# Block 1's stores of split weights: every other one issued by ScalarE instead of SyncE

## The chip, the cores and the metric

The kernel runs on one core of one Trainium2 chip. The metric is the device time of one execution in microseconds (us). Five engines work side by side, each through its own instruction stream in order: PE (TensorE, matmuls), DVE (VectorE), ACT (ScalarE), POOL (GpSimd) and SP (SyncE, which here does nothing but issue DMAs). DMAs can be issued from SP, ACT and POOL; they run on 16 DMA engines.

## The reference

```python
q_s = softmax of q over its 64 channels;  k_s = softmax of k over the 576 positions
kv  = einsum('bhsd,bhse->bhde', k_s, v)          # 8 batches x 8 heads, 64x64 each
x   = einsum('bhsd,bhde->bhse', q_s, kv)         # then laid out as (4608, 512)
xn  = x / sqrt(mean(x*x) + 1e-6) * rms_g
g   = xn @ w_gate;  val = xn @ w_val             # 512 -> 1536
out = (silu(g) * val) @ w_out                    # 1536 -> 512, float32
```

Inputs and output are float32: q, k and v of shape (8, 8, 576, 64), two weights of 512x1536 and one of 1536x512.

## The kernel before

The 4608 tokens are worked in nine blocks of 512. Blocks 0, 1 and 2 run one after the other with plain matrix products; the other six run as three pairs with Strassen products. In a plain block the hidden width of 1536 is cut into 12 chunks of 128. A chunk has a number s = 12 x block + i, so block 1 is s = 12 to 23. Steps of a chunk are `f1.s` (gate and value products, PE, line 973), `g_mul`, `silu`, `h_mul` (DVE, ACT, DVE), `h_hi` and `h_lo` (the split of the hidden values in two, ACT and POOL or DVE) and `f2.s` (the output product, PE, line 1010). Between them stand the steps of the attention of a later batch: `q_load`, `k_load`, `v_load` fetch a group of q, k or v (8, 3 and 5 DMAs), `q_max` to `q_x` are the softmax of q and its product with kv, `k_max` to `kv_lo` the softmax of k and kv.

Every float32 factor is split into a high and a low part, and a product is three products of parts. For the weights this is `w_hi`, `w_lo`, `o_hi`, `o_lo` (high parts are ACT casts, line 408; low parts are subtractions on POOL or DVE, lines 897 and 905). The split halves of a chunk lie in a ring of two tiles `w` (gate and value halves, 1 MB) and two tiles `o` (output halves, 512 KB). For the Strassen products sums of weight quarters S1 to S4 are made in block 1 also (`s_add.i.n`) and split (`s_hi`, `s_lo`, line 955) into a ring of three tiles `parts`.

In block 1 all these halves are written to DRAM, to be loaded back from block 2 on by POOL (`w_back`, `o_back`, `w_in`, `o_in`) in place of being split again: `w_keep.s` stores 1 MB (12 times), `o_keep.s` 512 KB (12 times) and `s_keep.i.n` 512 KB (24 times). They are the stores of the change. `r_keep` stores raw weights likewise and stays on SP.

What sets the order: a list of steps written out as text, `ORDER` (lines 22 to 341), worked through once by a loop at the end of the kernel. A step "name.arguments:engine" calls the function of that name; `unit[0]` is the engine that stands behind the colon, and `on(default)` gives it or the function's default. Each engine's stream is the list's order, cut to that engine's instructions. Nothing is reordered later; waits are put in from the tiles that an instruction reads and writes.

The DMAs of SP and of ACT count on eight semaphores, DMAHW0 to DMAHW7, handed out nearly in turn in the order of the list. An issuing instruction first waits until the DMA that used its semaphore last has landed. So no more than eight of these DMAs are under way, and a DMA on one engine can wait for one that the other engine has to issue. POOL's DMAs have semaphores of their own.

Of the kernel before, what the change touches and what calls it, by code (L numbers as in the profile page):

```python
# [90 lines left out]
kv_lo.2.0 w_lo.14.1:P f1.14.0 o_lo.15:D q_rec.2.1 s_lo.1.2:D k_tr.2.2 q_x.2.0 q_mul.2.1:P q_sum.2.3 k_top.2.2 o_keep.15
v_ones.2.3 s_add.0.1:D k_rows.2.2 f1.14.1 w_keep.14 q_t.2.1 q_mul.2.2:P v_load.2.3 q_hi.2.1:A s_add.2.1:D o_hi.13:A
k_sub.2.2 q_lo.2.1:P h_hi.13:A q_half2.2.3 s_hi.0.1:A q_x.2.1 o_lo.13:P w_hi.15.0.2:A q_sum2.2.3 q_rec.2.3 x_hi.2.1:A
s_add.2.2:D x_sq.2.0 x_lo.2.1 h_lo.13:P f2.13 x_hi.2.0:A g_mul.14 k_exp.2.2 o_keep.13 w_lo.15.0:P x_lo.2.0 s_hi.2.1:A
q_load.3.0 q_t.2.2 k_mm.2.2 q_mul.2.3:P k_max.2.3 q_hi.2.2:A x_sq.2.1 w_lo.15.1:P f1.15.0 q_t.2.3 silu.14 v_ones.3.0
s_lo.2.1:D s_lo.0.1:P h_mul.14 k_tr.2.3 s_keep.1.2 k_load.3.0 k_top.2.3 f1.15.1 h_hi.14:A s_add.0.3:D o_hi.14:A
q_lo.2.2:D w_hi.16.0.2:A w_keep.15 o_lo.14:P g_mul.15 s_keep.0.1 k_eps.2.2 r_keep.0 k_rec.2.2 kv_hi.2.2:A x_acc.2.1:D
o_keep.14 k_rows.2.3 h_lo.14:P f2.14 s_hi.2.2:A kv_lo.2.2 q_load.3.2 q_hi.2.3:A q_max.3.0 silu.15 w_lo.16.1:P k_sub.2.3
q_half.3.0 k_exp.2.3 w_lo.16.0:P f1.16.0 k_max.3.0 s_lo.2.2:P h_mul.15 q_max2.3.0 h_hi.15:A q_lo.2.3:P k_tr.3.0
w_hi.17.0.2:A q_x.2.2 k_top.3.0 g_mul.16 k_rows.3.0 s_hi.0.3:A w_lo.17.0:P f1.16.1 w_keep.16 s_keep.2.1 v_load.3.0  # L100
q_sub.3.0:D k_sub.3.0 q_exp.3.0 w_lo.17.1:D k_exp.3.0 k_mm.2.3 s_add.2.4:D x_sq.2.2 s_lo.0.3:D silu.16 h_lo.15:D f2.15
s_add.0.2:D q_max.3.2 x_hi.2.2:A s_add.0.4:P s_keep.2.2 q_sum.3.0 f1.17.0 o_hi.16:A s_keep.0.3 h_mul.16 o_hi.17:A
o_lo.16:P k_load.3.1 s_hi.0.4:A k_eps.2.3 q_half.3.2 w_hi.18.0.2:A o_lo.17:P k_rec.2.3 q_half2.3.0 kv_hi.2.3:A f1.17.1
q_sum2.3.0 x_lo.2.2 h_hi.16:A s_add.3.1:P o_keep.16 w_keep.17 q_rec.3.0 kv_lo.2.3 q_load.3.1 q_mul.3.0:P s_hi.3.1:A
g_mul.17 silu.17 k_mm.3.0 s_lo.0.4:P q_t.3.0 s_hi.0.2:A q_x.2.3 k_eps.3.0 v_ones.3.2 h_lo.16:D f2.16 k_max.3.1
w_lo.18.0:P x_hi.2.3:A x_lo.2.3 w_lo.18.1:P v_ones.3.1 s_lo.0.2:D f1.18.0 o_keep.17 k_rec.3.0 s_lo.3.1:P h_mul.17
s_keep.0.4 kv_hi.3.0:A k_load.3.2 h_hi.17:A x_acc.2.2:D h_lo.17:P x_sq.2.3 f1.18.1 g_mul.18 w_hi.19.0.2:A w_keep.18
s_keep.3.1 x_acc.2.3:D v_load.3.1 q_max.3.1 w_lo.19.0:P n_hi.2:A o_hi.18:A q_half.3.1 k_tr.3.1 silu.18 f2.17 o_lo.18:P
q_max2.3.1 s_hi.2.4:A k_top.3.1 h_mul.18 n_lo.2:P h_hi.18:A w_hi.20.0.2:A w_lo.19.1:D f1.19.0 kv_lo.3.0 s_add.2.3:P
w_keep.19 k_max.3.2 s_keep.0.2 h_lo.18:P s_hi.2.3:A o_keep.18 v_load.3.2 o_hi.20:A k_rows.3.1 w_lo.20.0:D k_tr.3.2  # L110
f1.19.1 k_sub.3.1 s_add.3.2:P g_mul.19 s_lo.2.4:P k_top.3.2 silu.19 n_sum.2 q_sub.3.1:P h_mul.19 k_rows.3.2 f2.18
h_hi.19:A w_lo.20.1:D k_exp.3.1 q_max2.3.2 n_t.2 s_keep.2.4 q_sub.3.2:P q_load.3.3 n_y0.2 o_lo.20:P n_y1.2 q_exp.3.1
f1.20.0 s_hi.3.2:A w_hi.21.0.2:A k_sub.3.2 o_hi.19:A w_lo.21.0:P q_sum.3.1 q_exp.3.2 k_mm.3.1 k_exp.3.2 q_half2.3.1
s_add.1.3:P w_keep.20 f1.20.1 q_hi.3.0:A o_keep.20 q_sum2.3.1 v_ones.4.0 s_add.4.3:D v_load.4.0 k_eps.3.1 o_lo.19:P
k_rec.3.1 g_mul.20 kv_hi.3.1:A k_mm.3.2 q_sum.3.2 h_lo.19:P silu.20 n_cols.1 f2.19 k_eps.3.2 q_half2.3.2 q_lo.3.0:P
k_rec.3.2 h_mul.20 w_lo.21.1:P q_sum2.3.2 kv_lo.3.1 h_hi.20:A o_keep.19 f1.21.0 kv_hi.3.2:A k_load.4.0 v_ones.3.3
s_lo.3.2:D w_hi.22.0.2:A n_rows.2 s_lo.2.3:P s_hi.1.3:A w_keep.21 q_max.3.3 o_hi.21:A q_rec.3.1 s_keep.2.3 h_lo.20:D
f1.21.1 s_keep.3.2 q_mul.3.1:P n_cols.2 k_load.3.3 q_half.3.3 w_lo.22.1:P q_max2.3.3 g_mul.21 q_t.3.1 w_lo.22.0:P f2.20
kv_lo.3.2 q_hi.3.1:A s_lo.1.3:D silu.21 w_keep.22 q_load.4.0 q_lo.3.1:D o_lo.21:D q_x.3.0 h_mul.21 f1.22.0 s_add.4.1:D
h_hi.21:A s_add.3.3:D w_hi.23.0.2:A h_lo.21:P s_hi.4.1:A o_hi.22:A q_sub.3.3:P q_x.3.1 g_mul.22 f1.22.1 k_max.3.3  # L120
o_lo.22:P silu.22 s_keep.1.3 x_sq.3.1 o_keep.21 k_max.4.0 x_sq.3.0 s_hi.3.3:A q_exp.3.3 q_rec.3.2 w_lo.23.0:D f2.21
s_lo.4.1:D x_acc.3.1:D s_keep.4.1 w_hi.24.0.2:A s_add.3.4:D v_load.3.3 w_lo.23.1:D s_hi.3.4:A f1.23.0 q_sum.3.3
s_add.5.3:P o_hi.23:A h_mul.22 q_half2.3.3 q_mul.3.2:P h_hi.22:A q_max.4.0 s_lo.3.4:P w_keep.23 f1.23.1 q_sum2.3.3
q_t.3.2 o_keep.22 q_half.4.0 q_hi.3.2:A q_load.4.1 s_add.5.1:P g_mul.23 q_lo.3.2:D h_lo.22:D f2.22 x_cp.3.0:A
w_lo.24.0:D x_cp.3.1:A o_lo.23:D silu.23 s_lo.3.3:D q_rec.3.3 k_tr.3.3 w_lo.24.1:D q_x.3.2 o_keep.23 s_hi.5.1:A
# [13 lines left out]
g_mul.27 f1.27.1 k_max.4.2 silu.27 k_load.4.3 v_ones.4.3 s_lo.4.4:P q_half2.4.2 v_load.4.3 n_lo.3:P k_eps.4.1 k_rec.4.1
q_t.4.1 kv_hi.4.1:A f2.26 w_lo.28.0:P h_mul.27 x_sq.4.0 kv_lo.4.1 q_hi.4.1:A s_lo.5.4:D o_hi.27:A h_hi.27:A q_sum2.4.2  # L140
w_lo.28.1:D s_keep.5.4 w_hi.29.0.2:A n_sum.3 q_max2.4.3 q_rec.4.2 q_load.5.1 q_sub.4.3:P k_tr.4.2 f1.28.0 k_top.4.2
n_t.3 q_mul.4.2:P q_exp.4.3 h_lo.27:D q_lo.4.1:P n_y0.3 s_hi.5.3:A k_rows.4.2 f1.28.1 k_sub.4.2 s_keep.4.4 o_lo.27:P
q_t.4.2 r_keep.3 k_exp.4.2 q_sum.4.3 q_load.5.0 w_lo.29.0:P q_half2.4.3 q_x.4.1 g_mul.28 w_back.30 f2.27 x_sq.4.1
k_max.4.3 s_lo.5.3:P x_cp.4.1:A silu.28 n_y1.3 w_lo.29.1:P s_keep.5.3 k_tr.4.3 f1.29.0 q_sum2.4.3 q_rec.4.3 h_mul.28
q_mul.4.3:P k_top.4.3 h_hi.28:A n_rows.3 o_hi.28:A h_lo.28:P q_t.4.3 o_hi.29:A k_mm.4.2 q_hi.4.2:A o_lo.28:P k_rows.4.3
k_eps.4.2 k_load.5.0 f1.29.1 g_mul.29 k_rec.4.2 k_sub.4.3 silu.29 x_nm.3.0:P kv_hi.4.2:A q_load.5.2 k_exp.4.3 kv_lo.4.2
v_ones.5.1 f2.28 q_max.5.0 w_back.31 q_lo.4.2:P q_half.5.0 q_hi.4.3:A q_max2.5.0 q_max.5.1 x_acc.4.1:P q_half.5.1
# [197 lines left out]
def linear_attention_then_gated_ffn(ctx: ExitStack, tc, q, k, v, w_gate, w_val, w_out, rms_g, out):  # L345
    nc = tc.nc
# [568 lines left out]
    def w_keep(s):  # L915
        i, odd = divmod(s % NF, 2)
        nc.sync.dma_start(parts_of(i, A21 if odd else A11, 2),
                          wh_[s].rearrange("p m a b f -> p m a (b f)").bitcast(F32))
# [508 lines left out]
```

## Time and profile before

| | us |
|---|---|
| median of three runs | 946.04 (943.25 to 947.05) |
| the profiled execution | 943.55 |
| its span, first to last instruction | 941.8 |
| busy: PE / DVE / ACT / POOL | 921.6 / 726.2 / 470.3 / 539.3 |
| block 1's stores lie between | 144 and 316 |

The profile is of one execution. Its span lacks 1.75 us of that execution's time, and that execution is 2.5 us below the median. The granted TensorE clock was 0.997 over the span. All numbers below are in us from the span's start unless said otherwise. "SPq" and "ACTq" are the issuing of DMAs on SP and ACT, which counts as no busy time.

### The profile page before, as it was taken

How to read it: one execution, taken by the hardware profiler on the slowest of the kernel's cores; microseconds unless marked ns; L12 is line 12 of the kernel's file. 1: busy time of each engine (PE TensorE's matmuls, PEld its weight loads, DVE VectorE, ACT ScalarE, POOL GpSimd, SP SyncE). 2: the span in 40 equal slices, each digit the busy share in tenths (PEclk: the TensorE clock that was granted, in tenths of full speed). 3: DMA queues.
4: the chain of work that ended last, by engine and by line, in shares of the span. 5: the costliest groups of instructions: out<-in, count | busy, mean ns of one | idle time of the engine just before them, and what ended most of it. 6: DMA issues, size and time to landing. Idle time of an engine off the chain costs nothing.

```text
span 941.8 us, 14388 instructions
## 1 busy us (share of the span) xinstructions
PE 921.6 (98%) x4625; PEld 748.3 (79%) x4625; DVE 726.2 (77%) x1525; ACT 470.3 (50%) x745; POOL 539.3 (57%) x531
## 2 busy tenths in 40 slices
...
GB/s 248 293 241 214 155 42 281 299 251 270 316 260 166 243 239 297 201 226 244 256 188 266 254 280 201 294 317 252 173 185 220 195 209 269 269 206 205 49 134 90
DMA packets 215463, 211.79 MB, mean 225 GB/s; under 512 B 139828, under 2 KB 176732, under 8 KB 210780
## 3 DMA queue, kind: packets, MB, share of 16 engines
...
q14 instruction: 38, 0.31, 0.1%
...
## 4 chain that ended last, share of the span: by engine, by line
PE 82%; DVE 5%; DMA 5%; SPq 4%; POOL 1%; issue 1%; ACT 1%; DVEq 0%; ACTq 0%; POOLq 0%
PE ps_gv L1122 18%; PE ps_gv L973 13%; PE ps_o L1122 12%; PE ps_o L1010 7%; PE ps_a L1122 7%; PE ps_o L1331 6%; PE ps_o L1215 4%; PE ps_a L1331 3%; PE ps_gv L1331 3%; DMA qt<-in_q_dram 2%; PE ps_a L1215 2%; PE ps_gv L1215 2%; PE ps_a L577 2%; PE ps_a L785 1%; DMA od<-o 1%
## 5 line engine op out<-in xcount | busy, mean ns | idle before, releaser
L973 PE MATMUL ps_gv<-xh,w 128*128 128x512 f32 x576 | 190.2, 397 | 3.6 <-DVE gs L985 2.9
L1122 PE MATMUL ps_gv<-x,ring 128*128 128x512 f32 x576 | 143.0, 393 | 0.0
L973 PEld LDWEIGHTS ps_gv<-xh,w 128*128 128x128 f32 x576 | 108.3, 188 | 28.8 <-DVE gs L985 4.1
L1122 PEld LDWEIGHTS ps_gv<-x,ring 128*128 128x128 f32 x576 | 107.0, 188 | 22.3
L973 PE MATMUL ps_gv<-xl,w 128*128 128x512 f32 x288 | 111.7, 391 | 0.0
L1143 DVE TENSOR_TENSOR tmp<-tmp,ps_gv 128x512 f32<-128x512 f32 x84 | 57.2, 683 | 47.8 <-PE ps_gv L1122 43.9
L1122 PE MATMUL ps_o<-x,ring 128*128 128x512 f32 x360 | 85.0, 390 | 0.0
L1095 POOL DMA_DIRECT2D ring<-wd x54 | 30.8, 570 | 88.9 <-PE ps_gv L1122 39.6
L1122 PEld LDWEIGHTS ps_o<-x,ring 128*128 128x128 f32 x360 | 67.6, 188 | 14.2
L1010 PE MATMUL ps_o<-o,hh 128*128 128x512 f32 x288 | 73.9, 398 | 0.1
L973 PEld LDWEIGHTS ps_gv<-xl,w 128*128 128x128 f32 x288 | 54.2, 188 | 10.6 <-issue 0.4
L1010 PEld LDWEIGHTS ps_o<-o,hh 128*128 128x128 f32 x288 | 52.7, 188 | 11.4 <-POOL o L905 0.4
L408 ACT CAST hh<-gs 128x512 fp32r<-128x512 f32 x50 | 30.8, 617 | 49.8 <-POOL gs L1287 19.7
L1143 DVE TENSOR_TENSOR tmp<-tmp,ps_o 128x512 f32<-128x512 f32 x42 | 28.7, 685 | 25.5 <-PE ps_o L1122 25.1
L897 POOL TENSOR_TENSOR w<-w,w 128x512 fp32r<-128x512 f32 x34 | 44.7, 1325 | 4.3 <-ACT w L408 2.4
L994 POOL TENSOR_TENSOR hl<-gs,hh 128x512 fp32r<-128x512 f32 x23 | 32.0, 1391 | 21.5 <-ACT hh L408 15.3
L534 DVE TENSOR_REDUCE cm<-kt 116x128 f32<-116x640 f32 x28 | 36.6, 1311 | 5.1 <-DMA kt<-in_k_dram 4.9
L1010 PE MATMUL ps_o<-o,hl 128*128 128x512 f32 x144 | 39.0, 393 | 0.0
L1122 PE MATMUL ps_a<-x,ring 128*128 128x512 f32 x144 | 37.0, 392 | 0.0
L1122 PE MATMUL ps_a<-x,w 128*128 128x512 f32 x144 | 36.7, 390 | 0.0
L1095 POOL DMA_DIRECT2D w<-wd x18 | 10.1, 562 | 45.5 <-PE ps_a L1122 35.7
L1122 PE MATMUL ps_gv<-x,w 128*128 128x512 f32 x144 | 35.1, 392 | 0.0
...
## 6 DMA issues: line engine op xcount, KB each, us to landing
...
```

The source lines that it names most:

```text
L408: (e.copy if e is nc.scalar else e.tensor_copy)(dst, src)
L534: nc.vector.tensor_reduce(out=cm, in_=kt_[b, g].rearrange("p h j d -> p h d j"), axis=AX.X, op=ALU.max)
L577: nc.tensor.matmul(pk[h * D:(h + 1) * D, :D + 1], lhsT=ke[:n, h, j], rhs=vt[:n, j, h], start=(j == 0), stop=(j == len(rows) - 1))
L897: on(nc.gpsimd).tensor_tensor(out=w[:, :, 1], in0=halves(s % NF, a, 1)[:, 0], in1=w[:, :, 0].bitcast(F32), op=ALU.subtract)
L973: nc.tensor.matmul(pd[s], lhsT=w[:, a, c // 2, m, c % 2 * P:c % 2 * P + P], rhs=X[j, c][x], start=(n == 1), stop=(n == 3 * NKT))
L994: on(nc.gpsimd).tensor_tensor(out=hl, in0=g_[s], in1=h_[s][0].bitcast(F32), op=ALU.subtract)
L1010: nc.tensor.matmul(po[t], lhsT=a[:, t * P:(t + 1) * P], rhs=w, start=(i == 0 and n == 0), stop=(i == NF - 1 and n == len(terms) - 1))
L1095: nc.gpsimd.dma_start(t, src.rearrange("p a b f -> p (a b f)"))
L1122: nc.tensor.matmul(abc[p, i, m, b], lhsT=src[:, h, c * P:(c + 1) * P], rhs=operand(o, c, x), start=first and n == 0, stop=n == 5, skip_gro ...
L1143: nc.vector.tensor_tensor(out=dst, in0=ux[u + (src,)], in1=abc[u + (b,)], op=ALU.add)
L1215: nc.tensor.matmul(pa[p, t, k], lhsT=a[:, k * P:(k + 1) * P], rhs=w, start=(c == 0 and n == 0), stop=(c == NF - 1 and n == 2))
L1331: nc.tensor.matmul(qacc[p, b, x], lhsT=ws[l][x], rhs=h[m], start=first and i == 0 and n == 0, stop=i == NH - 1 and n == 2, skip_group_chec ...
```

## The change

The engine table gets an entry for SP, the three store functions take the engine that their step names, and the 48 store steps of block 1 are tagged `:A` (ACT) and `:S` (SP) in turn. A tag moves the instruction into ACT's stream at the place of the step. 24 stores are ACT's now: 8 of `w_keep` (12, 14, 16, 18, 19, 20, 22, 23), 7 of `o_keep` (12, 16, 17, 18, 19, 21, 23) and 9 of `s_keep` (1.4, 1.2, 0.1, 2.2, 2.3, 3.4, 5.1, 4.2, 4.4), 16 MB of 30 MB together.

```diff
-    where = {"A": nc.scalar, "D": nc.vector, "P": nc.gpsimd, "": None}
+    where = {"S": nc.sync, "A": nc.scalar, "D": nc.vector, "P": nc.gpsimd, "": None}
...
     def w_keep(s):
         i, odd = divmod(s % NF, 2)
-        nc.sync.dma_start(parts_of(i, A21 if odd else A11, 2),
+        on(nc.sync).dma_start(parts_of(i, A21 if odd else A11, 2),
...
     def o_keep(s):
-        nc.sync.dma_start(od[s % NF], ot_[s].bitcast(F32))
+        on(nc.sync).dma_start(od[s % NF], ot_[s].bitcast(F32))
...
     def s_keep(i, n):
-        nc.sync.dma_start(parts_of(i, {1: S1, 2: S2, 3: S3, 4: S4}[n], 1)[:, :, 0],
+        on(nc.sync).dma_start(parts_of(i, {1: S1, 2: S2, 3: S3, 4: S4}[n], 1)[:, :, 0],
```

In `ORDER` the store steps and some loads stand at other places of the text, but the instructions of PE, DVE and POOL keep their order, and so do those of ACT apart from the stores that it gains. SP keeps the order of its loads; a few of the stores that it keeps stand one or two loads earlier or later. Line numbers of the changed kernel are one higher.

First place, SP before, from the store of chunk 14's output halves (od_113) over the eight DMAs of `q_load.3.2` to the stores of `w_keep.16` and `s_keep.2.1` (both wd_107):

```order
L1231 DMA rd_123<-w_92 256x1x512 [waits DMAHW7_49]
L921 DMA od_113<-o 128x1024 [waits DMAHW0_49,Pool_49]
L647 DMA qt<-in_q_dram 32x6x32 [waits DMAHW1_49,DVE_49]
...
L647 DMA qt<-in_q_dram 32x10x32 [waits DMAHW6_49]
L647 DMA qt<-in_q_dram 32x10x32 [waits DMAHW7_49]
L647 DMA qt<-in_q_dram 32x10x32 [waits DMAHW0_49]
L917 DMA wd_107<-w 128x2x1024 [waits DMAHW1_49,Activation_49,Pool_49]
L958 DMA wd_107<-parts 128x2x512 [waits DMAHW2_49,DVE_49]
L523 DMA vt<-in_v_dram 112x5x64 [waits DMAHW3_49]
```

The same place of SP in the change:

```order
L1232 DMA rd_123<-w_92 256x1x512 [waits DMAHW0_49]
L922 DMA od_113<-o 128x1024 [waits DMAHW1_49,Pool_49]
L648 DMA qt<-in_q_dram 32x6x32 [waits DMAHW3_49,DVE_49]
...
L648 DMA qt<-in_q_dram 32x10x32 [waits DMAHW7_49]
L648 DMA qt<-in_q_dram 32x10x32 [waits DMAHW0_49]
L648 DMA qt<-in_q_dram 32x10x32 [waits DMAHW1_49]
L648 DMA qt<-in_q_dram 32x10x32 [waits DMAHW2_49]
```

And ACT there in the change, where `w_keep.16` and `s_keep.2.2` (wd_107) now stand:

```order
L983 ACTIVATE gs<-gs 128x512
L570 ACT_TABLE_LOAD [waits DMAHW7_49,DMAHW6_49]
L570 ACTIVATE kt<-kt 116x640 [waits DVE_49]
L918 DMA wd_107<-w 128x2x1024 [waits DMAHW7_49,Activation_49,Pool_49]
L409 CAST hh<-gs 128x512 [waits DVE_49]
L959 DMA wd_107<-parts 128x2x512 [waits DMAHW2_49,Pool_49]
L409 CAST w<-w_94 128x4x256 [waits DMAHW6_49,PE_49]
```

Before, the 1 MB store stood on SP behind the q load, and `s_keep.2.2` further back behind a v load. Now both are ACT's, ahead of its cast `hh`. They use DMAHW7 and DMAHW2, and the q load's fifth and eighth DMA wait on these two semaphores; before, the eighth waited for the store od_113.

Second place, ACT in the change around `s_keep.4.4` (wd_109), behind the silu of chunk 27:

```order
L983 ACT_TABLE_LOAD
L983 ACTIVATE gs<-gs 128x512 [waits DVE_49]
L959 DMA wd_109<-parts 128x2x512 [waits DMAHW5_49,Activation_49,Pool_49]
L414 ACTIVATE kv<-ps_a,rs 64x64 [waits DVE_49,PE_49]
L414 ACTIVATE kv<-ps_a,rs 64x64
```

And SP in the change at the three DMAs of `k_load.4.3`, the v load behind them, a store and the first of `q_load.5.1`:

```order
L526 DMA vt<-in_v_dram 1x2x64 [waits DMAHW3_49]
L499 DMA kt<-in_k_dram 112x2x320 [waits DMAHW4_49,PE_49,Activation_49]
L499 DMA kt<-in_k_dram 3x2x320 [waits DMAHW5_49]
L500 DMA kt<-in_k_dram 1x10x64 [waits DMAHW6_49]
L524 DMA vt<-in_v_dram 112x5x64 [waits DMAHW7_49]
...
L959 DMA wd_110<-parts 128x2x512 [waits DMAHW4_49,DVE_49,Activation_49]
L648 DMA qt<-in_q_dram 32x10x32 [waits DMAHW5_49,Pool_49]
```

The store takes DMAHW5 on ACT, and the second DMA of the k load, SP's, is the next to use it. Before, `s_keep.4.4` stood on SP, behind `q_load.5.1` and ahead of `q_load.5.0`.

More of the change, by code (lines that the diff above doesn't have):

```diff
@@ L91 @@
[L91 to L125, printed above, removed]
@@ L126 @@
-q_mul.3.3:P q_max2.4.0 k_top.3.3 s_keep.3.3 f1.24.0 h_mul.23 x_cp.3.2:A s_keep.3.4 q_sub.4.0:P x_sq.3.2 q_t.3.3
-o_hi.24:A q_load.4.2 q_hi.3.3:A o_lo.24:P w_hi.25.0.2:A k_rows.3.3 g_mul.24 k_tr.4.0 f1.24.1 k_top.4.0 silu.24
+s_lo.1.1:P s_hi.1.4:A q_sum.2.2 k_exp.2.1 o_lo.12:P q_half.2.3 silu.12 k_mm.2.1 w_keep.13:S g_mul.13 v_load.2.2
+s_lo.1.4:P q_max2.2.3 q_half2.2.1 f1.13.1 o_keep.12:A k_eps.2.1 h_mul.12 q_lo.2.0:P store.0.3:A k_rec.2.1 q_half2.2.2
+q_sub.2.3:P k_eps.2.0 q_sum2.2.1 q_sum2.2.2 q_rec.2.2 k_rec.2.0 s_keep.1.1:S k_load.2.3 store.0.1:A s_keep.1.4:A
@@ new lines @@
+x_lo.2.0 s_hi.2.1:A q_t.2.2 k_mm.2.2 o_keep.13:S q_mul.2.3:P k_max.2.3 q_hi.2.2:A q_load.3.0 x_sq.2.1 w_lo.15.1:P
+f1.15.0 q_t.2.3 silu.14 v_ones.3.0 s_lo.2.1:D s_lo.0.1:P h_mul.14 k_tr.2.3 k_top.2.3 f1.15.1 h_hi.14:A s_add.0.3:D
+s_keep.0.1:A q_lo.2.2:D k_load.3.0 o_hi.14:A g_mul.15 w_hi.16.0.2:A o_lo.14:P k_eps.2.2 k_rec.2.2 kv_hi.2.2:A
+w_keep.15:S k_rows.2.3 x_acc.2.1:D r_keep.0 s_hi.2.2:A kv_lo.2.2 h_lo.14:P f2.14 o_keep.14:S q_hi.2.3:A q_load.3.2
+q_max.3.0 silu.15 k_sub.2.3 w_lo.16.1:P q_half.3.0 k_exp.2.3 w_lo.16.0:P f1.16.0 k_max.3.0 s_lo.2.2:P h_mul.15
@@ new lines @@
+w_keep.17:S h_hi.16:A q_mul.3.0:P kv_lo.2.3 q_load.3.1 o_keep.17:A g_mul.17 s_hi.3.1:A s_lo.0.4:P q_t.3.0 silu.17
+k_mm.3.0 s_hi.0.2:A v_ones.3.2 q_x.2.3 w_lo.18.0:P k_eps.3.0 x_hi.2.3:A h_lo.16:D f2.16 k_max.3.1 w_lo.18.1:P x_lo.2.3
+v_ones.3.1 w_keep.18:A s_lo.3.1:P f1.18.0 s_keep.0.4:S k_load.3.2 s_lo.0.2:D k_rec.3.0 h_mul.17 kv_hi.3.0:A x_acc.2.2:D
+h_hi.17:A f1.18.1 g_mul.18 x_sq.2.3 h_lo.17:P w_hi.19.0.2:A s_keep.3.1:S v_load.3.1 x_acc.2.3:D q_max.3.1 w_lo.19.0:P
+n_hi.2:A k_tr.3.1 f2.17 o_hi.18:A q_half.3.1 silu.18 o_lo.18:P q_max2.3.1 s_hi.2.4:A k_top.3.1 h_mul.18 n_lo.2:P
```

117 lines of the change are left out of this document (71 added, 46 removed).

## The prediction

> **What bounds the kernel now.** I read the page first, then the waits of PE between 130 and 330 us, where the moved stores lie.
>
> ```profile
> PE 921.6 (98%) x4625; PEld 748.3 (79%) x4625; DVE 726.2 (77%) x1525; ACT 470.3 (50%) x745; POOL 539.3 (57%) x531
> ```
> ```profile
> PE ps_gv L973 <- DVE gs L985: 2.9, 3, 2.3
> PE ps_a L577 <- DMA vt<-in_v_dram: 1.1, 1, 1.1
> PE ps_a L835 <- DVE kt L565: 1.0, 1, 1.0
> PE ps_a L549 <- DVE cm L534: 0.4, 1, 0.4
> PE ps_a L785 <- DVE kv L621: 0.3, 1, 0.3
> PE ps_gv L973 <- DVE gs L978: 0.2, 1, 0.2
> ```
>
> PE is busy for all but 20 us of the span, so the kernel is PE-bound. The second table (microseconds in total, times, longest) says what PE waited for in the 200 us that the change touches: 5.9 us together. That is all that a better order of DMAs can win. A loss has no such limit: PE stops when a load comes late.
>
> The next views are the stages in windows of 10 us and the issuing of stores. The columns of the first are PE, PEld, DVE, ACT and POOL busy, clock, share of the DMA engines, GB/s.
>
> ```profile
> 180.00:190.00 10.00, 10.00 (x52) 8.18 (x52) 8.93 (x19) 8.18 (x13) 8.31 (x6) 1.00 0.96 336
> 190.00:200.00 10.00, 9.09 (x56) 7.23 (x56) 6.16 (x19) 4.94 (x8) 6.62 (x6) 1.00 0.77 229
> 250.00:260.00 10.00, 7.74 (x34) 6.08 (x33) 8.21 (x17) 6.55 (x10) 4.83 (x5) 1.00 0.94 310
> ```
> ```profile
> L917 SPq DMA_DIRECT2D wd<-w x12: 372/394/422, 144.2 to 261.4; - x12
> L921 SPq DMA_DIRECT2D od<-o x12: 340/392/1344, 160.6 to 268.4; - x12
> L958 SPq DMA_DIRECT2D wd<-parts x24: 372/408/950, 162.4 to 315.5; - x24
> L1377 ACTq DMA_DIRECT2D out_dram<-res x16: 374/521/891, 918.7 to 937.0; - x16
> ```
>
> A store costs SP about 0.4 us of its queue (minimum, median, maximum in ns). PE loses its time in the stages where the DMA engines are at 0.94 to 0.96 or just behind them. So two things are short, SP's queue and the DMA engines, and the change relieves only the first.
>
> **What the change removes.** 24 issues leave SP: 15 of 0.39 us and 9 of 0.41 us make 9.5 us over 144 to 316 us. SP serves its list in order, so the loads behind a store are issued that much earlier, where nothing else holds them. The loads are what PE's waits go back to: 1.1 us straight to a v load, and the waits for DVE in part to k loads:
>
> ```profile
> DVE cm L534 <- DMA kt<-in_k_dram: 4.5, 3, 2.9
> ```
>
> I take 1.5 us as won, about half of PE's 2.9 us for `gs`. The bounds are 5.9 us won, and 3 us lost if other q and k loads of 200 to 260 us meet what the next part finds at 185 us.
>
> **What it adds on ACT.** 24 issues of 0.39 to 0.52 us (the SP and the ACT rows above) take 9.5 to 12.5 us of ACT's stream. ACT is half idle and none of PE's six waits names it, and it waits itself for late stores:
>
> ```profile
> ACT parts L408 <- DMA wd<-parts: 12.8, 8, 4.2
> ACT w L408 <- DMA wd<-w: 4.4, 3, 2.5
> ```
>
> These 17.2 us wait for a tile that a store still reads. Stores that leave earlier shorten them. I charge 0.5 us, with 0 and 2 as bounds; the cover is ACT's idle time, and without it the price would be the whole 9.5 to 12.5 us.
>
> **What it moves, first place.** Around 185 us SP's queue and the chain of waits show this:
>
> ```profile
> 183.16 8.68 DMA od<-o
> 191.85 0.31 SPq L647
> ```
> ```profile
> 184.59 7.57 SPq L647 DMA_DIRECT2D qt<-in_q_dram  x8
> 192.27 0.40 SPq L917 DMA_DIRECT2D wd<-w  x1
> 198.45 0.89 SPq L958 DMA_DIRECT2D wd<-parts  x2
> ```
> ```profile
> 184.72 0.74 ACT L569 ACTIVATE kt<-kt 116x640 f32<-116x640 f32 x1
> 185.36 0.60 ACT L408 CAST hh<-gs 128x512 fp32r<-128x512 f32 x1
> 185.87 1.04 ACT L408 CAST w<-w 128x1024 fp32r<-128x1024 f32 x1
> ```
>
> The eighth DMA of the q load was issued only when a store of 512 KB had landed, 8.68 us after its start: it uses that store's semaphore. The chain goes on from there to the v load. In the change `w_keep.16` goes out when ACT has come to its place behind the exponential at 184.72, between 184.7 and 185.5, where SP sent it at 192.27. `s_keep.2.2` goes out at about 185.9, where SP sent it at 198.45 (the first of the two). So 1.5 MB (1.57 million bytes) move 7 and 12 us ahead, into the stage whose DMA engines are at 0.96. At that stage's 336 GB/s they are 4.7 us of transfers, beside or ahead of the q load and of the store before it, and the fifth and eighth DMA of the q load now wait for them by their semaphores. What is late next:
>
> ```profile
> 193.71 0.69 DVE L713 TENSOR_REDUCE st<-qt 128x16 f32<-128x512 f32 x1 [1.99 <-DMA qt<-in_q_dram]
> 200.18 0.89 PE L577 MATMUL ps_a<-vt,kt 116*64 116x65 f32 x20 [1.09 <-DMA vt<-in_v_dram]
> ```
>
> DVE already waits 1.99 us for this q load, and PE 1.09 us for the v load that SP issues behind it. Neither has slack. If the q load ends 4.7 us later, the v load gains back 0.5 us (one store less ahead of it, 192.27 to 192.77) at the least, and the 3.1 us of transfer of the 1 MB store, now gone earlier, at the most: 4.2 or 1.1 us late. It could be 0 if the stores yield to the loads. I take 3.0 us, nearer to the upper end because DVE, in whose stream the q load's maximum stands ahead of PE's operand `gs`, has no gain from the v load. The range is 0 to 4.2.
>
> A rule speaks against the change here. The Trainium skill ("DMA: Bandwidth & Descriptors", section "Issuing engines are not separate DMA queues") says that DMAs of all issuing engines run on the same 16 engines and interleave, and that issuing from several saves only the issue time. By it nothing beyond the 9.5 us of SP's queue can come out well, and the transfers brought forward still have to be served; the share of 0.96 agrees, and the sum by it stays as it is.
>
> **What it moves, second place.** Around 300 us:
>
> ```profile
> 299.37 0.64 ACT L982 ACTIVATE gs<-gs 128x512 f32<-128x512 f32 x1
> 300.44 0.63 ACT L413 ACTIVATE kv<-ps_a,rs 64x64 fp32r<-64x64 f32 x2 [0.43 <-DVE rs L601]
> ```
> ```profile
> 298.02 0.73 SPq L498 DMA_DIRECT2D kt<-in_k_dram  x2
> 309.98 5.43 SPq L647 DMA_DIRECT2D qt<-in_q_dram  x8
> ```
> ```profile
> 201.50 3.24 DMA kt<-in_k_dram
> 213.75 4.55 DMA wd<-w
> 310.71 7.40 DMA qt<-in_q_dram
> 318.19 0.31 SPq L498
> ```
>
> `s_keep.4.4` stands behind the silu, which starts at 299.37 and ends at 300.0; the store goes out at 300.0 at the latest. Its 512 KB lie between a k load of 280 KB (3.24 us from issue to landing) and a 1 MB store (4.55), so it lands at about 303.5. The second DMA of `k_load.4.3`, which now waits for its semaphore, started before half through the pair that begins at 298.02, at 298.4. SP stands still for 5.1 us. It no longer issues that store itself (0.4), so `q_load.5.0` starts 4.7 us later than 309.98. Who waits:
>
> ```profile
> 328.83 0.69 DVE L713 TENSOR_REDUCE st<-qt 128x16 f32<-128x512 f32 x1 [0.64 <-issue]
> 332.20 0.68 DVE L994 TENSOR_TENSOR hl<-gs,hh 128x512 fp32r<-128x512 f32 x1
> 332.98 1.16 PE L1010 MATMUL ps_o<-o,hl 128*128 128x512 f32 x4
> ```
> ```profile
> 310.53 0.89 POOL L925 DMA_DIRECT2D w<-wd  x1 [0.47 <-POOL w L897]
> 322.61 5.21 DMA qt<-in_q_dram
> ```
>
> The chain of waits leads from this q load over its landing at 318.11 to SP's next k load (318.19) and q load (322.61), and to DVE's maximum at 328.83. Behind that in DVE's stream stands the low part `hl`, which ends at 332.88, and PE takes it up 0.1 us later. So PE has no slack. But the two q loads took 7.40 and 5.21 us while a 1 MB load of POOL (310.53) ran beside them; if it is that load that sets their landing, a part of the 4.7 us is swallowed. I take 3.0 us, some two thirds; the bounds are 0.5 and 4.7.
>
> The last store of the change lies at 315.5 (the L958 row), so nothing that it moved is left after that; a loss further back could only be handed on.
>
> **The sum.** -1.5 + 0.5 + 3.0 + 3.0 = +5.0 us. On the profiled execution's 943.55 us (span 941.8 and 1.75 around it) this is 948.6; that execution stands 2.5 us below the median of 946.04, and on the median it is **951.0**. All terms at their good ends give -5.9 + 0 + 0 + 0.5 = -5.4 (940.6), all at their bad ends 3 + 2 + 4.2 + 4.7 = +13.9 (959.9). Ends do not fall together, so the range is **943.0 to 958.0**, and the likeliest case's own is 948.5 to 954.
>
> **Rivals.** *The relief of SP wins.* SP's queue is what binds the loads, the transfers brought forward fit in the gaps (0.77 at 190 to 200), and PE gets most of its 5.9 us back. It decides if `q_load.3.2` ends no later than 194 and the k load at 298 does not wait. Price: -1.0 (the ACT issues and a rest of waits) from 5.9 gives -4.9, so 941.1. For it: SP issues back to back from 180 to 200. Against it: SP's own wait at 191.85 was for a landing, not for the queue. The Trainium skill ("Perfetto Trace Analysis", section "DMA Optimizations") says that balancing over the issuing engines may help where issuing is the bottleneck; the 0.96 share says that at 185 it is not alone.
>
> *The gains and losses cancel.* The 1 MB load of POOL sets the landing of the two q loads (0.5 in place of 3.0), the v load gains back most (1.1 in place of 3.0), and SP's relief is worth its 1.5: -1.5 + 0.5 + 1.1 + 0.5 = +0.6, so 946.6. For it: the long landings of 7.40 and 5.21. Against it: no slack at DVE or PE in either place.
>
> *Both waits in full.* Each semaphore shared by the two engines passes on its wait, 4.2 and 4.7, and one more of the q loads at 200 to 260 us does so too, 3, with 0.5 on ACT: +12.4, so 958.4. The point from which it decides is the landing of ACT's stores: 4 us or more after their issue. For it: od<-o took 8.68 in a full stage. Against it: a store that comes earlier also frees ACT's tiles earlier.
>
> **How the numbers follow.** About 0.5%, 4.7 us, is what a measurement of this kernel can tell from no change. The forecast has 0.40, the full waits 0.12, cancelling 0.30, the relief 0.18. The forecast's own range reaches from +2.5 to +8, so some of it, 0.08, falls within 0.5%; from cancelling as much as 0.03 goes to either side; of the relief 0.05 stays within. Slower by over 0.5%: 0.40 - 0.08 + 0.12 + 0.03 = 0.47. Faster: 0.18 - 0.05 + 0.03 = 0.16. Same: 0.37.
>
> **What would show it.** Right: SP's eighth DMA of the q load at 185 to 192 starts after 193, later than 191.85; PE's wait for the v load at 200 us grows beyond 1.09 us; the k load near 298 us stops for about 5 us behind its first DMA; PE waits for `hl` near 335 us by 2 to 4 us. Right also: ACT's waits for wd<-parts fall well below 12.8 us, and its issues last 0.4 to 0.5 us. Wrong: these loads start as before or earlier, and PE's waits of 130 to 330 us sum to less than 5.9 us; then the relief decides. Wrong in another way: PE waits for ACT, which no row shows now, or a loss in a stage without moved stores.

## The result and the profile after

| | before | after |
|---|---|---|
| median of 12 runs each | 944.09 (942.46 to 947.05) | 950.78 (947.70 to 956.17) |
| ratio, 95% interval | | 1.0066 (1.0049 to 1.0084) |
| the profiled execution | 943.55 | 948.21 |
| its span | 941.8 | 946.4 |
| granted TensorE clock over the span | 0.997 | 0.994 |

The change makes the kernel 0.66% slower, 6.2 us by the ratio. The profiled execution is one of its shorter ones, 2.6 us below the median, so its trace shows where the loss arises but not its usual size.

First the page of the changed kernel, the busy times:

```profile
PE 922.5 (97%) x4625; PEld 748.6 (79%) x4625; DVE 727.3 (77%) x1525; ACT 470.8 (50%) x745; POOL 538.6 (57%) x531
```

PE does the same work (0.9 us more busy), so what was lost is waiting, and a little clock. Next the waits of PE between 130 and 345 us (total, times, longest):

```profile
PE ps_gv L974 <- DVE gs L986: 4.2, 3, 2.2
PE ps_a L578 <- ACT kt L570: 2.3, 1, 2.3
PE ps_o L1011 <- DVE hl L995: 1.2, 1, 1.2
PE ps_a L550 <- DVE cm L535: 1.1, 1, 1.1
PE ps_a L786 <- ACT sq L803: 0.2, 1, 0.2
PE ps_gv L974 <- DVE gs L979: 0.2, 1, 0.2
```

Together 9.2 us, where the six rows before came to 5.9. The wait for the v load is gone. Two rows are new: 2.3 us for ACT's exponential of k, and 1.2 us for `hl`. The waits of SP (140 to 345 us) and of ACT (130 to 330 us) say who was late:

```profile
SPq L648 <- DMA wd<-w: 8.9, 4, 3.2
SPq L959 <- DMA wd<-parts: 4.5, 2, 2.7
SPq L499 <- DMA wd<-parts: 4.0, 1, 4.0
SPq L500 <- DMA wd<-parts: 3.7, 1, 3.7
```
```profile
ACT parts L409 <- DMA wd<-parts: 14.6, 5, 4.0
```

SP's loads (L648 is a q load, L499 and L500 a k load) and two of its own stores (L959) stand in front of stores: they need a semaphore on which a store still counts. SP, from which 24 issues were taken to make it faster, now stands still for stores, 21.1 us in these four rows; before, the one such row was of 0.8 us.

**Where the time went, place by place.** A pair of traces can be read by pairing the instructions of PE, whose order is the same, and taking the start in the one less the start in the other. For the changed kernel against the kernel before PE is late by (us):

| at (us) | 170 | 180 | 195 | 206 | 226 | 262 | 330 | 340 | end |
|---|---|---|---|---|---|---|---|---|---|
| PE late by | -0.1 | 2.4 | 2.4 | 5.0 | 3.5 | 2.8 | 2.9 | 4.3 | 4.5 |

There are three jumps: 2.5 us at 175, 2.5 us at 200, 1.4 us at 335. Between the second and the third 2.1 us come back. The stages in windows of 10 us (columns as in the prediction: PE, PEld, DVE, ACT, POOL busy, clock, share of the DMA engines, GB/s; the share adds up the time of packets and can pass 1):

```profile
170.00:180.00 10.00, 7.27 (x46) 5.29 (x46) 6.69 (x11) 7.80 (x12) 6.67 (x7) 1.00 0.75 227
200.00:210.00 10.00, 9.00 (x51) 7.04 (x52) 7.86 (x22) 5.17 (x9) 6.20 (x7) 0.83 0.96 324
250.00:260.00 10.00, 9.83 (x46) 7.91 (x44) 6.17 (x9) 5.62 (x9) 2.87 (x4) 1.00 0.72 226
260.00:270.00 10.00, 8.58 (x39) 6.90 (x40) 9.73 (x26) 7.31 (x12) 6.58 (x6) 1.00 0.98 319
330.00:340.00 10.00, 8.56 (x41) 6.61 (x40) 7.75 (x18) 5.78 (x10) 6.01 (x7) 1.00 1.23 285
```

PE is idle for 2.7 us in the first of these windows and for 1.4 us in the last. In the second a clock of 0.83 adds 1.7 us to the idle time of 1.0. The third is the stage in which PE was busy for only 7.74 us before. PE comes to that place 3.5 us later now, so most of its wait there lies in the fourth window: it was 2.3 us and is 1.6. That gives back 0.7 of the 2.1 us; the other 1.5 came back between 206 and 226.

**The first jump, not foreseen.** The chain of waits of the changed kernel, in order of time, with ACT's cast from the timeline behind it:

```profile
157.42 7.61 DMA wd<-parts
165.04 0.02 SPq L959
165.09 5.78 DMA wd<-parts
170.89 0.05 ACT parts L409
```
```profile
170.89 0.62 ACT L409 CAST parts<-sums 128x512 fp32r<-128x512 f32 x1 [2.40 <-DMA wd<-parts]
```

`s_keep.1.4`, now ACT's, took 7.61 us to land. SP's next store, `s_keep.1.1`, needed its semaphore and left only at 165.09; ACT needed the tile which that store reads, and waited 2.40 us for it to land. Behind the cast stands the exponential of k, for which PE waited 2.3 us.

**The second jump** is the prediction's first place. SP's q load there, and two rows of the chain:

```profile
186.84 10.46 SPq L648 DMA_DIRECT2D qt<-in_q_dram  x8
```
```profile
187.79 9.07 DMA wd<-parts
196.88 2.01 DMA qt<-in_q_dram
```

The eight DMAs took 10.46 us to go out, where they took 7.57 before. The longest hold was at the fifth: it stood 3.2 us for `w_keep.16` (the longest wait of SP's first row above) and went out at 195.49. `s_keep.2.2` went out at 187.79 on ACT and landed 9.07 us later; then only could the eighth DMA of the q load start, at 196.88 (191.85 before), but for this one SP stood only some 0.1 us more.

**The third jump** is the second place. SP's and POOL's issues (the times are of the start, then the length until the last of the group), and DVE's maximum behind the last of these q loads:

```profile
300.86 4.63 SPq L499 DMA_DIRECT2D kt<-in_k_dram  x2
315.98 5.44 SPq L648 DMA_DIRECT2D qt<-in_q_dram  x8
324.12 4.10 SPq L648 DMA_DIRECT2D qt<-in_q_dram  x8
```
```profile
323.53 0.77 POOL L926 DMA_DIRECT2D w<-wd  x1 [1.47 <-PE ps_gv L974]
```
```profile
333.08 0.69 DVE L714 TENSOR_REDUCE st<-qt 128x16 f32<-128x512 f32 x1 [2.04 <-DMA qt<-in_q_dram]
```

The pair of k DMAs that took 0.73 us before takes 4.63: the second waits 4.0 us for `s_keep.4.4` (the L499 row above). The last q load then starts 0.59 us after POOL's 1 MB load, where before it started 0.96 us ahead of it:

```profile
319.73 4.14 SPq L647 DMA_DIRECT2D qt<-in_q_dram  x8
320.69 0.77 POOL L925 DMA_DIRECT2D w<-wd  x1 [1.44 <-PE ps_gv L973]
```

DVE waits 2.04 us for it, and PE 1.2 us for `hl`, which stands behind in DVE's stream. SP had come to its second k DMA at 301.2, ACT sent `s_keep.4.4` only at 302.24, and it landed 3.0 us later: a quarter of SP's 4.0 us went by before ACT had issued the store.

### The profile page after: what moved, and what is told of

Its sections match the earlier page's. It is cut to its first block, busy times and chain, and to the rows that moved or that the text cites. A ratio compares the mean times of both kernels' runs of the same rounds, so it can differ in the third digit from the quotient of the medians.

```text
span 946.4 us, 14363 instructions
## 1 busy us (share of the span) xinstructions
PE 922.5 (97%) x4625; PEld 748.6 (79%) x4625; DVE 727.3 (77%) x1525; ACT 470.8 (50%) x745; POOL 538.6 (57%) x531
## 4 chain that ended last, share of the span: by engine, by line
PE 80%; DMA 9%; DVE 4%; SPq 3%; ACT 2%; issue 1%; POOL 1%; ACTq 0%; DVEq 0%; POOLq 0%
PE ps_gv L1123 17%; PE ps_gv L974 13%; PE ps_o L1123 12%; PE ps_a L1123 7%; PE ps_o L1011 7%; PE ps_o L1332 6%; PE ps_o L1216 3%; PE ps_a L1332 3%; DMA wd<-parts 3%; PE ps_gv L1332 3%; DMA qt<-in_q_dram 2%; PE ps_a L1216 2%; PE ps_gv L1216 2%; PE ps_a L578 1%; DMA kt<-in_k_dram 1%; DMA wd<-w 1%
## 5 line engine op out<-in xcount | busy, mean ns | idle before, releaser
L995 POOL TENSOR_TENSOR hl<-gs,hh 128x512 fp32r<-128x512 f32 x23 | 32.0, 1390 | 18.7 <-ACT hh L409 12.4
```

The lines of the kernel that those rows point to most:

```text
L995: on(nc.gpsimd).tensor_tensor(out=hl, in0=g_[s], in1=h_[s][0].bitcast(F32), op=ALU.subtract)
```

## The experiments

All were timed in five rounds, 6 to 12 runs of each; the kernel before was run beside them each time, and the ratios are to those runs. Its medians there were 944.99 (the first four kernels), 945.97 (the next four), 945.31 (the late store alone, ten small DMAs, three stores behind loads) and 945.64 (five small DMAs). Names are of steps in `ORDER`; a diff shows the steps of the list that differ, one to a line.

### Which part of the change costs

**The four stores of the three places back to SP.** Against the change:

```diff
-s_keep.1.4:A
+s_keep.1.4:S
...
-w_keep.16:A
+w_keep.16:S
...
-s_keep.2.2:A
+s_keep.2.2:S
...
-s_keep.4.4:A
+s_keep.4.4:S
```

> The change with four of its stores given back to SP at the same places of the list: s_keep.1.4, w_keep.16, s_keep.2.2 and s_keep.4.4; the other 20 stay on ACT. Theory (the loss lies in single waits of SP for stores that ACT has to issue, at these four): PE's jumps of 2.3 us at 175, 2.4 at 201 and 1.4 at 337 go away, the gain of about 3 us between 201 and 260 stays; 6 us less than the change, so 942 to 945, no slower than before. Rival (ACT's 24 issues cost ACT time that PE waits for): 20 of 24 issues stay, so five sixths of the loss stay, about 949. Rival (two queues share the DMA engines badly, whichever store it is): about 949 also.

Measured: 946.14, ratio 1.0011 (0.9996 to 1.0027). With 20 of the 24 stores still on ACT the loss is gone, and the gain of about 3 us that the expectation had does not show.

**All 24 stores back to SP**, in the changed list:

```diff
-w_keep.12:A
+w_keep.12:S
...
-s_keep.4.4:A
+s_keep.4.4:S
```

> The change's list with all 48 stores issued by SP: only the places of the list are the change's. Theory: no wait of SP for a store of ACT is left, but stores that the list has pulled forward (s_keep.1.2 and w_keep.16 among them) stand ahead of loads on SP; 943 to 947. Rival (the places in the list make the loss, not the engine): as the change, 950 to 951.

Measured: 945.99, ratio 1.0016 (0.9995 to 1.0037). So the list's other edits, by which some stores and loads stand elsewhere in SP's stream, do not make the loss, and the 20 harmless stores on ACT are worth nothing that can be measured (1.0011 against 1.0016).

**Only the first place on ACT**: the list of the last experiment with two stores on ACT.

```diff
-w_keep.16:S
+w_keep.16:A
...
-s_keep.2.2:S
+s_keep.2.2:A
```

> The list of the change with all stores on SP but w_keep.16 and s_keep.2.2, which ACT issues. Theory (two stores of ACT hold the q load at 185 to 197): PE's jump near 200 is there, 2 to 2.5 us, and those at 175 and 337 are not; 2 us over the kernel with all stores on SP. Rival (many issues on ACT are needed for a loss): the same time as with all stores on SP, within 0.7 us.

Measured: 945.29, ratio 1.0005 (0.9982 to 1.0028). The first place alone costs nothing that shows at the end; up to 2.6 us lie within the interval.

**ACT's time without the stores**: all stores on SP, and at the 24 places a copy on ACT, which is work added.

```diff
+    pad = const.tile([P, P], F32, name="pad")
...
+    def act_pad(n):
+        nc.scalar.copy(pad, ones)
...
-w_keep.12:A
+w_keep.12:S act_pad.0
...
```

> All 48 stores on SP, and at each of the 24 places of ACT's stores a copy of 128x128 values to a tile that nobody reads, 0.2 to 0.4 us of ACT each: the price of ACT's time alone, with no store moved. Theory: 0 to 1 us over the kernel with all stores on SP. Rival (ACT's time is what the change pays with): 4 to 6 us over it.

Measured: 944.93, ratio 1.0006 (0.9987 to 1.0026). The copies took somewhat less than an issue, by the groups of this kernel and of the changed kernel (minimum, median, maximum in ns):

```profile
L918 ACT COPY pad<-ones x24: 278/293/301, 146.1 to 300.4; 128x128 f32<-128x128 f32 x24
```
```profile
L918 ACTq DMA_DIRECT2D wd<-w x8: 366/375/507, 144.2 to 260.2; - x8
L959 ACTq DMA_DIRECT2D wd<-parts x9: 366/366/421, 157.4 to 302.2; - x9
```

24 copies of 0.293 us are 7.0 us of ACT's stream against about 8.7 us for the issues (24 at 0.36). They cost nothing, so the time that ACT spends on issuing isn't the loss.

**One place given back at a time.** Against the change, each of these alone:

```diff
-s_keep.1.4:A
+s_keep.1.4:S
```

> The change with s_keep.1.4 alone given back to SP at its place of the list. Theory: SP's s_keep.1.1 no longer stands for 2.7 us on a semaphore that an ACT store uses, ACT's cast gets its tile, and PE's wait for the exponential of k at 175 us (2.3 us) goes; the others stay. 1.5 to 2.5 us less than the change, about 948.5. If delays are absorbed behind (waits at 200 to 260 take up what came late before), less: 0 to 1 us.

```diff
-s_keep.4.4:A
+s_keep.4.4:S
```

> The change with s_keep.4.4 alone given back to SP. Theory: SP's k load near 301 us no longer stands for 4 us, PE's wait for the low part near 337 us (1.2 us) goes; 1 to 2 us less than the change, about 949.3. Rival (the long landings of the q loads beside POOL's 1 MB load make that wait): within 0.5 us of the change.

```diff
-w_keep.16:A
+w_keep.16:S
...
-s_keep.2.2:A
+s_keep.2.2:S
```

> The change with w_keep.16 and s_keep.2.2 given back to SP. Theory: the q load at 187 to 197 us is issued without the stand of 3 us, PE's jump of 2.4 us at 201 goes; up to 2.5 us less than the change, about 948.3. Rival (a late start at 201 only shortens the waits that follow to 260 us): 0 to 1 us less, as two such stores alone cost nothing against all stores on SP.

| given back | median | ratio, 95% interval |
|---|---|---|
| nothing (the change) | 950.78 | 1.0066 (1.0049 to 1.0084) |
| `s_keep.1.4` (175 us) | 952.46 | 1.0072 (1.0045 to 1.0099) |
| `w_keep.16`, `s_keep.2.2` (200 us) | 951.09 | 1.0059 (1.0033 to 1.0085) |
| `s_keep.4.4` (335 us) | 946.47 | 1.0015 (0.9995 to 1.0036) |

One store of 24 makes the loss, as far as it stands clear of noise: `s_keep.4.4`. Given back, it wins 4.8 us by the ratios, more than the 1 to 2 us expected. (It was not run as the only store on ACT in the changed list.) The other two jumps are in the trace, 2.5 us each, and giving either back wins nothing that shows. SP's other waits for stores are still there with `s_keep.4.4` back (140 to 345 us):

```profile
SPq L648 <- DMA wd<-w: 9.2, 4, 3.2
SPq L959 <- DMA wd<-parts: 4.4, 2, 2.6
SPq L500 <- DMA wd<-parts: 3.5, 1, 3.5
```

These 17.1 us of standing cost the kernel nothing that shows (at most 3.4 us by the interval), and the 4.0 us at one k load cost it the loss. So not how long SP stands decides, but what is due behind it. PE's waits of 300 to 360 us with `s_keep.4.4` back, then the `hl` row with `s_keep.1.4` back and with the first place back:

```profile
PE ps_a L786 <- ACT sq L803: 0.2, 1, 0.2
```
```profile
PE ps_o L1011 <- DVE hl L995: 4.6, 1, 4.6
```
```profile
PE ps_o L1011 <- DVE hl L995: 3.4, 1, 3.4
```

Without the late store the wait is gone. Where an early jump is given back it is still there, 4.6 and 3.4 us in place of 1.2. It goes with the outcome of a race of two loads (start of SP's last q load and of POOL's load beside it; the last four rows are kernels described above and below):

| kernel | SP's q load | POOL's 1 MB load | q load ahead by | DVE waits for it | PE waits for `hl` |
|---|---|---|---|---|---|
| before | 319.73 | 320.69 | 0.96 | 0 (0.64 of issue) | 0 |
| `s_keep.4.4` back | 322.17 | 323.34 | 1.17 | 0 (0.40 of issue) | 0 |
| change | 324.12 | 323.53 | -0.59 | 2.04 | 1.2 |
| first place back | 319.26 | 318.55 | -0.71 | 4.25 (put down to a k load) | 3.4 |
| `s_keep.1.4` back | 323.03 | 322.24 | -0.79 | 5.48 | 4.6 |
| list of the change, all on SP | 323.23 | 323.19 | -0.04 | 1.33 (put down to a k load) | 0.5 |
| copies on ACT, all on SP | 322.75 | 321.96 | -0.79 | 5.23 | 4.8 |
| ten small DMAs, all on SP | 323.55 | 320.84 | -2.71 | 4.38 | 5.7 |
| five small DMAs, all on SP | 323.20 | 323.96 | 0.76 | 0.96 (put down to a k load) | 0 |

In the five profiles that are not in the table the q load is ahead by 0.64 to 2.07 us, and PE waits 0.2 us at most. So in all fourteen the sign says whether PE waits for `hl` by more than 0.2 us, and behind POOL's load the wait grows with the distance. POOL's load follows PE (its row names a product of PE): PE's lateness at 300 us taken off, it starts at 320.7 in every profile. The q load, taken the same way, starts at 321.3 to 321.5 in the three profiles of the table with `s_keep.4.4` on ACT and at 319.7 before. An early jump moves both sides alike, so giving it back leaves the last race nearly as it was (0.59, 0.71 and 0.79 us behind). For the same reason the profiles can't tell a q load that POOL's load slows from one that is simply too late for PE: no run moved POOL's load alone.

The rows behind the second line of the table, SP and POOL with `s_keep.4.4` back on SP:

```profile
300.67 0.70 SPq L499 DMA_DIRECT2D kt<-in_k_dram  x2
322.17 4.12 SPq L648 DMA_DIRECT2D qt<-in_q_dram  x8
```
```profile
323.34 0.77 POOL L926 DMA_DIRECT2D w<-wd  x1 [1.46 <-PE ps_gv L974]
```

The k pair goes out in 0.70 us, and the q load is ahead of POOL's load again.

### Is it the tie, or the transfers that come early?

**The four stores on POOL.** POOL's DMAs count on semaphores of their own, so the bytes move as early as in the change and SP isn't tied to them. Against the change:

```diff
-s_keep.1.4:A
+s_keep.1.4:P
...
-w_keep.16:A
+w_keep.16:P
...
-s_keep.2.2:A
+s_keep.2.2:P
...
-s_keep.4.4:A
+s_keep.4.4:P
```

> The change with the four stores s_keep.1.4, w_keep.16, s_keep.2.2 and s_keep.4.4 issued by POOL: they go out at the same early time on a third queue, but POOL's DMAs have semaphores of their own, so that SP waits for none of them. Theory (the shared semaphores make the loss): as with the four on SP, 944 to 947. Rival (the transfers brought forward crowd the loads, whoever issues them): as the change, 949 to 951. POOL's own price is up to 1 us each for four issues.

Measured: 947.01, ratio 1.0009 (0.9992 to 1.0027). The issues on POOL:

```profile
L959 POOL DMA_DIRECT2D wd<-parts x3: 742/757/901, 159.7 to 300.9; - x3
```

The last of them, `s_keep.4.4`, left at 300.9, where ACT's left at 302.24; measured against PE, which was 2.9 us late there in the change and 0.4 us here, POOL's was about 1 us the later. PE had no wait for `hl`. Nearly the same transfers without the tie: no loss. That speaks for the semaphore and against the load on the DMA engines.

**The late store alone on ACT**, in the list of before. Against the kernel before (the store's function takes the engine of the step, as in the change):

```diff
-k_eps.4.1 k_rec.4.1
+k_eps.4.1 s_keep.4.4:A k_rec.4.1
...
-k_sub.4.2 s_keep.4.4 o_lo.27:P
+k_sub.4.2 o_lo.27:P
```

> The kernel before with s_keep.4.4 alone issued by ACT, at its place in ACT's stream of the change. Here its semaphore falls on DMAHW3, whose next user on SP is the last DMA of the v load, six DMAs behind the k load's second one, which waited in the change. Theory (what costs is how long SP stands, that is how near the waiting DMA is): SP would have come there at 302.4 and the store lands at about 303.5, so it stands for about 1 us, less the 0.4 of the store that it no longer issues: 0 to 1.5 us over the kernel before. Rival (any ACT issue of this store costs the 5 us): 949 to 951.

Measured: 945.81, ratio 1.0000 (0.9984 to 1.0016). ACT's store, and SP's k pair and the DMA that follows the store on its semaphore:

```profile
300.49 0.40 ACTq L958 DMA_DIRECT2D wd<-parts  x1
```
```profile
299.77 0.73 SPq L498 DMA_DIRECT2D kt<-in_k_dram  x2
304.45 0.61 SPq L525 DMA_DIRECT2D vt<-in_v_dram  x1
```

In this list the numbers fall otherwise: the store gets DMAHW3, and the next to use it is the last DMA of `v_load.4.3`, six DMAs of SP later. SP comes to it 4.0 us after the store's issue, and was hardly held: from the k pair's start to this DMA are 4.68 us, and 4.40 us before (302.42 less 298.02). Store and engine are those of the change; the DMA that has to wait is another (and the list is that of before), and it costs nothing.

**SP held at that place, no store moved.** Ten (and in a second kernel five) DMAs of 16 bytes, work that is added, stand on SP ahead of `k_load.4.3`. Against the kernel before:

```diff
+    late = tc.dram_tile([P, P], F32, name="late")
+
+    def sp_late(n):
+        for x in range(n):
+            nc.sync.dma_start(late[x:x + 1, 0:4], ones[x:x + 1, 0:4])
...
-silu.27 k_load.4.3
+silu.27 sp_late.10 k_load.4.3
```

> The kernel before, all stores on SP, with ten DMAs of 16 bytes issued by SP ahead of k_load.4.3, which hold SP for 3.5 to 4 us at 298 and move next to no data: the stand of SP without any store on ACT. Theory (SP late at this place lets the q load at 320 fall behind POOL's 1 MB load, which then sets its landing, and PE waits for the low part at 337): 3.5 to 6 us over the kernel before, 948.5 to 951, with a PE wait of 3 us or more at 337. Rival (lateness of SP is absorbed behind, what costs is the store itself on ACT's queue): 0 to 1 us over it.

```diff
-silu.27 k_load.4.3
+silu.27 sp_late.5 k_load.4.3
```

> As the run before with ten small DMAs on SP ahead of k_load.4.3, but five of them: SP is held for 1.5 us at 298 instead of 3.0. Theory (a race: the second q load starts at 319.7 in the kernel before, POOL's next 1 MB load at 320.7; what SP issues after that lands 5 us later): 1.5 us put the whole q load behind POOL's load, PE waits 2 to 5 us for the low part at 337; 2 to 5 us over the kernel before. Rival (the loss is in proportion to the lateness): 4.5 us, half of what ten cost. Rival (1.5 us fit into slack): 0 to 0.7 us.

Measured: with ten 954.41, ratio 1.0096 (1.0073 to 1.0119); with five 947.65, ratio 1.0021 (1.0000 to 1.0043). SP with ten, and PE's waits of 300 to 360 us:

```profile
298.00 3.03 SPq L919 DMA_DIRECT2D late<-ones  x10
301.15 0.71 SPq L498 DMA_DIRECT2D kt<-in_k_dram  x2
323.55 7.21 SPq L647 DMA_DIRECT2D qt<-in_q_dram  x8
```
```profile
PE ps_o L1016 <- DVE hl L1000: 5.7, 1, 5.7
PE ps_a L785 <- ACT sq L802: 1.0, 1, 1.0
```

SP is held 3.03 us with no store on ACT, and PE's wait for `hl` is there, even longer. So a late SP at this spot is enough; the loss is larger than the 3.5 to 6 us expected. With five (1.58 us held) the profile shows no wait for `hl`, for the q load is still 0.76 us ahead of POOL's, and the interval reaches to 1.0000: not decided. Whatever slack there is at this spot is used up by 3.03 us.

### Where is the relief of SP?

**Three stores of before behind the loads that follow them**, all on SP. Against the kernel before:

```diff
-w_keep.19 k_max.3.2 ... v_load.3.2
+k_max.3.2 ... v_load.3.2 w_keep.19
...
-s_keep.2.3 ... w_keep.22 q_load.4.0
+... q_load.4.0 s_keep.2.3 w_keep.22
```

> The kernel before, all stores on SP, with three of them moved behind a load: w_keep.19 behind v_load.3.2, s_keep.2.3 and w_keep.22 behind q_load.4.0. These orders stand in the change's list, and PE's start came 1.2 us earlier near 221 and 2.4 us near 258 in every kernel that has them, with all stores on SP too. Theory: the gain between 200 and 260 us is one of the order on SP and needs no ACT: 2 to 3.6 us less than before, about 942. Rival (the gain is SP's relief by ACT): as before, within 0.7 us.

Measured: 947.35, ratio 1.0017 (0.9999 to 1.0035). No gain at the end. PE becomes later by 3.4 us between 226 and 240 us (from 1.23 to 4.64; half of it is a clock of 0.83 there) and gets 1.0 back by 262. Loads that stand earlier in SP's order are not worth 1.5 us here.

## Why the prediction was right, and where it was wrong

The forecast was slower, +5.0 us, 951.0; measured was slower, +6.2 us by the ratio (6.7 between the medians), 950.78. That the two times agree to 0.2 us is partly luck: the kernel before was 1.95 us faster in these runs than in the three shown, and the parts of the sum do not come out as the sum has them. By the medians `s_keep.4.4` makes (0.0066 - 0.0015) x 944 = 4.8 us, and everything else 1.4 us (interval -0.5 to 3.4). The 4.8 us can be some 2.6 us more or less by the two intervals.

**The relief of SP, -1.5: not shown.** In the trace 2.1 us come back between 206 and 262 us, 0.7 of them at PE's wait for `gs` near 258. But in the list of the change with all stores on SP PE gets 2.6 us back at that place (late by 4.8 at 256 and by 2.2 at 262), so this needs no ACT. None of the kernels with all or nearly all stores on SP, or with twenty or twenty-three on ACT and without the late one, is measurably faster or slower than the kernel before: ratios from 1.0000 to 1.0017. The step failed in taking a wait of PE behind a load for time that an earlier issue wins.

**ACT's issues, +0.5: nothing.** They took 0.36 to 0.38 us, below the 0.39 to 0.52 us taken, and copies of 7.0 us in their places cost nothing. The reason given for the small charge held in part: ACT's waits for a store's landing fell from the 17.2 us of the two rows to 14.6, since those for wd<-w are gone. Those for wd<-parts did not fall, as the prediction had it, but rose from 12.8 to 14.6 us; at the place shown, at 165 us, because a store on SP now waits for a store on ACT.

**First place, +3.0: right in the trace, not found at the end.** The eighth DMA of the q load started after 193, as said, at 196.88, and PE lost 2.5 us at 200 us. It showed not in the v load's wait, which vanished, but in DVE's `gs`, the stream that the prediction had weighed higher: DVE waited 4.9 us for the q load, where it was 2.0. The step that failed is taking this delay as the price at the end. Given back, the first place won nothing that shows (1.0059, 1.0033 to 1.0085, against 1.0066), nor did it cost anything alone that shows (1.0005, at most 2.6 us by its interval). The same holds for the jump at 175 us, which the prediction lacked altogether: it looked for SP's loads that wait for ACT's stores, and this is a store on SP that waits for one. Of the 5.0 us of both jumps 2.9 are still there at 330 us in the profile, and the profile with `s_keep.4.4` back ends 2.6 us later than the one before. The medians have 1.4 us for all of this, and whether any of it is real stays open.

**Second place, +3.0: the right mechanism, too small.** SP stood 4.0 us at the k load where 5.1 us were worked out, the q loads came late, and PE waited for `hl` (1.2, 3.4 and 4.6 us in three profiles; 2 to 4 were named). Worth 4.8 us by the medians. Three things stand behind the size.

The first is the late start. Of the 4.0 us the last q load keeps 1.6 us: from the start of the k pair to its own start are 23.26 us (324.12 less 300.86) and were 21.71 (319.73 less 298.02). The rest goes into the pause of SP that the prediction had quoted as the row at 318.19, between the store of 315.50 and the next k load. In that the rival of cancelling was right. In the changed kernel's profile this is all: DVE's maximum starts 9.0 us after the q load's first issue, as before (9.1), and PE waits 1.2 us.

The second is the race. 1.6 us is more than the 0.96 us by which the q load was ahead of POOL's load. At 0.71 and 0.79 us behind that load (first place and `s_keep.1.4` back) the maximum starts 11.0 and 12.2 us after the first issue, and PE waits 3.4 and 4.6 us. That POOL's load makes the difference is argued, not shown.

The third is the clock. Windows with the first place back, and with SP held by ten DMAs:

```profile
330.00:340.00 10.00, 6.59 (x23) 4.95 (x22) 8.76 (x21) 5.35 (x8) 4.65 (x5) 0.83 0.81 210
```
```profile
330.00:340.00 10.00, 3.33 (x17) 2.49 (x17) 5.47 (x15) 3.55 (x5) 1.84 (x3) 0.94 1.18 261
340.00:350.00 10.00, 10.00 (x49) 7.81 (x51) 7.20 (x19) 5.84 (x9) 7.31 (x8) 0.72 0.24 63
```

After the wait of 3.4 us the granted clock is 0.83 in the window, a loss of 1.7 us; the two make 5.1 us, and PE's lateness grew there by 5.2 (from -2.1 to 3.1). After the wait of 5.7 us the clock is 0.72 in the next window, 2.8 us more, and the lateness grew by 8.6 (from 0.9 to 9.6). The prediction priced the wait alone. In the changed kernel's own profile the wait was 1.2 us and the clock stayed 1.00 there, and this run is below the median. Its longer runs do have the lower clock: the five of 953 us and more have 0.988 to 0.992 over the span, the seven shorter ones 0.991 to 0.995. That they lose it at this place is argued from the two kernels, not shown. The Trainium skill ("TensorE: Matmul & The Clock Gate", section "What's actually happening") describes a gate that halves the clock after an idle window of about 3.4 us until a busy one has passed. Half speed for 3.4 us would be the 1.7 us of the 0.83 window, so the size agrees. When it comes does not go by the length of a wait here: the 0.83 of the changed kernel at 200 to 210 us stands behind a wait of 2.2 us, while a wait of 2.3 us at 256 before, and one of 3.3 us at 199 with the first place alone on ACT, were followed by none.

**The rivals.** The relief did not win. Cancelling would have been right but for one store: with `s_keep.4.4` back the time is 946.47 where that rival had 946.6, though by another sum. The waits in full had as their point a landing of ACT's stores 4 us or more after the issue. They landed 7.6 and 9.1 us after it at 157 and 188, but the one that made the loss landed 3.0 us after it. SP stood for 3.2 and 4.0 us where that rival passes on 4.2 and 4.7, and only the second shows in the time.

**A correction to the text on the kernel before.** The eight semaphores are not handed out in the order of the list. In the change `k_load.4.3` stands ahead of `s_keep.4.4` there, and still its second DMA waits on the store's semaphore. The store is given its number eight DMAs ahead of that one, and ACT comes to issue it later than SP comes to its load. That ACT would get to its place late was what the prediction saw; why a load that stands ahead in the list must wait for it could only be read from the waits that the instructions carry.

**What stays open.** Why 3.03 us of SP held cost 9.1 us and the 4.0 us of the tie 4.8. With ten small DMAs the last q load starts 3.7 us later against PE than before, so nothing of the hold is taken up, and with the tie 1.6. It took 7.21 us to issue in place of 4.10, 2.7 us behind the start of the 1 MB load (323.55 against 320.84) in place of 0.59. Why the wait jumps from 1.2 to 4.6 us between 0.59 and 0.79 us behind isn't shown, and each of these is one execution. The race isn't safe without the change either: the kernel with the copies on ACT, whose median is the lowest of all these, was profiled in its longest run, 952.23, with a wait of 4.8 us for `hl`.
